# Top-k attention and a SmeLU MLP on one core: paired top-k, earlier exponentials, SmeLU off VectorE

## The chip, the cores and the metric

The kernel runs on one core of a Trainium2 chip, in one launch. The metric is the device time of that launch in microseconds (us). The engines are named as in the profile: PE (TensorE), PEld (its weight loads), DVE (VectorE), ACT (ScalarE), POOL (GpSimd) and SP (SyncE, which only issues transfers here).

## The reference

Eight batches of eight heads, 576 positions, head size 64. For every query the 32 largest scores are kept, a softmax is taken over them, and the result is multiplied by the values. The heads are put side by side (4608 tokens of 512) and go through a two-layer MLP with SmeLU between:

```
scores = q @ k.T / sqrt(64)
kth    = 32nd largest of each row;  mask = scores >= kth
attn   = exp(where(mask, scores, -1e9) - max);  attn /= sum(attn) + 1e-9
x      = (attn @ v), heads side by side            # 4608 x 512
h      = x @ w_in                                  # 512 x 2048
g      = h if h >= 1, 0 if h <= -1, else (h + 1)^2 / 4
out    = g @ w_out                                 # 2048 x 512
```

q, k and v are float32. The two weight matrices come as float64, and the kernel turns their 64-bit words into float32 on the chip.

## The kernel before

**Steps.** The attention is cut into 144 steps. A step is one tile of 128 query rows for two heads, so it holds two score blocks of 128 x 576 (tile `s`, i = 0 and 1). The leftover 64 rows of each head are paired into tail steps of the same size. Step m passes through `scores` (PE matmuls into PSUM, four ACT copies to `s`), `top_k` (DVE: four rounds of MAX8 and between them three of MATCH_REPLACE8, on each of the two blocks, 576 wide), `weights` (POOL makes the negated 32nd value `nkth` and a bias `nb`; ACT masks with a steep Prelu, then Exp with a running sum `z`; DVE adds 1e-9 and takes the reciprocal `rz`; POOL multiplies by it), `transpose_w` (PE transposes, ACT copies to `wT`) and `values` (PE, then an ACT copy to `xT`).

**The MLP.** Query tiles are gathered into chunks of two (sometimes one). When a chunk's attention is done, `mlp` puts 16 pieces `hidden(f)` and, for each tile, 8 pieces `final` into a list. `hidden(f)` makes `ph` in PSUM (3 buffers), then ACT makes r = relu(h/2 + 1/2), POOL squares it, and DVE writes g = min(max(h, 1), r^2), reading `ph`. `r` has 2 buffers. `final` accumulates g @ w_out in `py`.

**Weights.** `weight_piece` turns 512 columns at a time of float64 words into float32: three DVE operations, two on ACT, two on POOL, and a last one on DVE (line 98). 32 pieces are needed, three in each step from the start; a `hidden` or `final` piece may be issued only when the columns that it reads have been converted.

**Order.** PE's order is written out by hand: in iteration m the loop issues `values(m-2)`, `scores(m+1)`, half of the step's share of MLP pieces, `transpose_w(m-1)`, and the other half. The share is the MLP work that is left over the steps that are left. The order of the other engines is chosen by a scheduler when the program is built; each engine then runs its own list strictly in order, and waits on semaphores for the others and for itself.

Of the kernel before, what the change touches and what calls it, by code (L numbers as in the profile page):

```python
# [16 lines left out]
TOP_K = 32  # L17
# [4 lines left out]
def kernel(  # L22
# [29 lines left out]
    FAR = 2.0 ** 80  # L52
    PER_STEP = 3

    const = ctx.enter_context(tc.tile_pool(name="const", bufs=1))
    xtp = ctx.enter_context(tc.tile_pool(name="xtp", bufs=3))
    stage = ctx.enter_context(tc.tile_pool(name="stage", bufs=2))
    att = ctx.enter_context(tc.tile_pool(name="att", bufs=2))
    ps = ctx.enter_context(tc.tile_pool(name="ps", bufs=1, space=PSUM))

# [3 lines left out]
    nc.gpsimd.memset(half, 0.5)  # L64
    w_in = const.tile([P, NK, DFF], F32, name="w_in")
# [10 lines left out]
    WC = 512  # L76

    def weight_piece(pool, dst, src):
# [5 lines left out]
        top = pool.tile([P, WC], U32, name="top")  # L84
# [10 lines left out]

        size = pool.tile([P, WC], F32, name="size")
        nc.scalar.activation(size, hi.bitcast(F32), AF.Abs)
        nc.vector.scalar_tensor_tensor(out=dst, in0=size, scalar=1.125 * 2.0 ** -15, in1=low,  # L98
                                       op0=ALU.is_ge, op1=ALU.mult)

    def weight_pieces(pool):
        for c in range(0, DFF, WC):
            for kk in range(NK):
                weight_piece(pool, w_in[:, kk, c:c + WC], moe_w_in[kk * P:(kk + 1) * P, c:c + WC])
                yield
        for f in range(NF):
            for c in range(0, DM, WC):
                weight_piece(pool, w_out[:, f, c:c + WC], moe_w_out[f * P:(f + 1) * P, c:c + WC])
                yield
# [4 lines left out]
    def whole(x, b):  # L114

        return x[b, :, 0:SM, :].rearrange("h (p c) d -> p h c d", c=NT)

    def load_values(b):
        v_in = stage.tile([P, H, NT, D], F32, name="v_in")
        nc.sync.dma_start(out=v_in, in_=whole(v, b))  # L120
        v_tl = v_tails[b % 2]
        for j in range(2):
            nc.sync.dma_start(out=v_tl[0][j * TL:(j + 1) * TL, j::2, :],
                              in_=v[b, j::2, SM:S, :].rearrange("h p d -> p h d"))
        for hp in range(NHP):
            g = hp % 2
            nc.sync.dma_start(out=v_tl[1][g * TL:(g + 1) * TL, 2 * hp:2 * hp + 2, :],
                              in_=v[b, 2 * hp:2 * hp + 2, SM:S, :].rearrange("h p d -> p h d"))
        return v_in, v_tl

    def load_queries(b, t):
        if t < NT:
            q_in = stage.tile([P, H, D], F32, name="q_in", bufs=2)
            nc.sync.dma_start(out=q_in, in_=whole(q, b)[:, :, t, :])
        else:
            q_in = stage.tile([TL, H, D], F32, name="q_tl", bufs=2)
            nc.sync.dma_start(out=q_in, in_=q[b, :, SM:S, :].rearrange("h p d -> p h d"))
# [247 lines left out]
    for got in keys_of(0):  # L385
        keys[0] = got
# [78 lines left out]
```

## Time and profile before

| | us |
|---|---|
| median of 3 runs (lowest, highest) | 2017.13 (2016.01, 2020.04) |
| the profiled execution, its span | 2018.67, 2016.9 |
| busy: PE, PEld | 1717.6, 1175.6 |
| busy: DVE, ACT, POOL | 1608.3, 1075.0, 537.6 |

The profile is of one execution. Busy time is the union of an engine's instructions, and instructions of DVE, ACT and POOL overlap their neighbours a little, so what an instruction costs in a queue is the distance from its start to the next one's start. The view of waits and the `<-` at the end of a row name what ended the idle time in front of an instruction.

### The profile page before, as it was taken

Reading aid. Unit: us, or ns where it says so; the run is one execution under the profiler, and the core shown is the slowest. Engines: PE = TensorE matmul, PEld = TensorE weight load, DVE = VectorE, ACT = ScalarE, POOL = GpSimd, SP = SyncE. Lnnn points to the kernel's source line nnn. Section 1 sums busy time; section 2 is a strip of 40 time slices with the busy share of each in tenths; the row PEclk is TensorE's granted clock in tenths of the full one; section 3 lists DMA queues with packets and bytes.
Section 4 is the critical chain, followed back from the end, with each engine's and each line's share of the span. In section 5 each row is a group of like instructions: output and inputs, shape, how many; then the busy total and the mean of one; then the engine's idle time right before and its main releaser. Section 6 shows DMA issues by size and latency. Waiting matters only on the chain.

```text
span 2016.9 us, 29329 instructions
## 1 busy us (share of the span) xinstructions
PE 1717.6 (85%) x10128; PEld 1175.6 (58%) x10128; DVE 1608.3 (80%) x3648; ACT 1075.0 (53%) x2589; POOL 537.6 (27%) x1003
## 2 busy tenths in 40 slices
PE   3245488989989999989898999888999999998999
PEld 2243266557566666656565666656474765765666
DVE  4878789989897887889786887888787787968861
ACT  4545546565555654565555555565454555545442
POOL 2564522213221221213121222213131231321321
PEclk7667798999999999989998999999999999999999
DMA  6232200100011001100011000110010000000000
GB/s 162 78 92 75 68 14 18 41 22 12 21 30 30 22 3 29 33 22 11 21 30 29 22 1 23 28 35 11 14 33 21 17 6 11 6 16 6 1 11 11
DMA packets 102803, 57.45 MB, mean 28 GB/s; under 512 B 85760, under 2 KB 93952, under 8 KB 102656
## 3 DMA queue, kind: packets, MB, share of 16 engines
q1 hardware_dynamic: 102656, 55.59, 10.0%
q8 instruction: 80, 1.31, 0.3%
q14 instruction: 67, 0.55, 0.1%
HBM read 46.14 MB, written 9.44 MB: 28 GB/s over the span
## 4 chain that ended last, share of the span: by engine, by line
DVE 53%; PE 19%; ACT 12%; POOL 10%; issue 6%; DMA 1%; SPq 0%; POOLq 0%; DVEq 0%; ACTq 0%
DVE tops L218 27%; DVE rest L221 20%; PE py L315 9%; PE ph L300 4%; ACT s L228 4%; ACT s L239 3%; DVE g L307 3%; POOL s L244 3%; ACT s L209 2%; POOL r L306 2%; PE sp L206 2%; POOL low L93 2%; PE po L269 2%; POOL low L94 2%; PE pw L254 2%
## 5 line engine op out<-in xcount | busy, mean ns | idle before, releaser
L300 PE MATMUL ph<-xT,w_in 128*128 128x256 f32 (+1 forms) x2816 | 560.4, 355 | 72.0 <-DVE g L307 71.8
L218 DVE MAX8 tops<-rest 128x8 f32<-128x576 f32 x864 | 619.5, 748 | 0.1
L315 PE MATMUL py<-w_out,g 128*128 128x512 f32 x1152 | 558.6, 630 | 45.1 <-DVE w_out L98 39.5
L300 PEld LDWEIGHTS ph<-xT,w_in 128*128 128x128 f32 x2816 | 466.2, 197 | 158.0 <-DVE g L307 87.9
L221 DVE MATCH_REPLACE8 rest<-tops,rest 128x576 f32<-128x576 f32 x576 | 424.1, 743 | 0.0
L315 PEld LDWEIGHTS py<-w_out,g 128*128 128x128 f32 x1152 | 217.5, 199 | 306.1 <-issue 238.0
L228 ACT ACTIVATE s<-s,nkth 128x576 f32<-128x576 f32 x288 | 214.4, 772 | 315.4 <-POOL nkth L233 315.2
L218 DVE MAX8 tops<-s 128x8 f32<-128x576 f32 x288 | 205.9, 750 | 202.7 <-ACT s L209 202.7
L244 POOL TENSOR_SCALAR s<-s,rz 128x576 f32<-128x576 f32 x288 | 217.6, 768 | 382.0 <-DVE rz L242 243.1
L306 POOL TENSOR_TENSOR r<-r 128x256 f32<-128x256 f32 (+1 forms) x352 | 187.8, 540 | 423.6 <-ACT r L304 418.4
L206 PE MATMUL sp<-kT,qT 64*128 64x288 f32 x1024 | 196.8, 452 | 60.2 <-ACT xT L282 51.2
L304 ACT ACTIVATE r<-ph,half 128x256 f32<-128x256 f32 (+1 forms) x352 | 148.2, 433 | 172.8 <-PE ph L300 141.3
L255 ACT COPY wT<-pw 128x512 f32<-128x512 f32 x288 | 155.9, 587 | 132.8 <-PE pw L254 131.7
L239 ACT ACTIVATE s<-s,nb 128x576 f32<-128x576 f32 x288 | 221.6, 770 | 1.2
L254 PE MATMUL pw<-ident,s 128*128 128x128 f32 x1152 | 163.5, 288 | 68.8 <-POOL s L244 64.1
L209 ACT ACTIVATE s<-sp 128x288 f32<-128x288 f32 x576 | 198.7, 410 | 36.3 <-PE sp L206 34.7
L221 DVE MATCH_REPLACE8 rest<-tops,s 128x576 f32<-128x576 f32 x288 | 212.6, 743 | 0.0
L254 PEld LDWEIGHTS pw<-ident,s 128*128 128x128 f32 x1152 | 142.9, 149 | 119.5 <-POOL s L244 72.6
L307 DVE SCALAR_TENSOR_TENSOR g<-ph,r 128x256 f32<-128x256 f32 (+1 forms) x352 | 128.6, 368 | 76.4 <-POOL r L306 71.3
L233 POOL TENSOR_SCALAR nkth<-tops 128x2 f32<-128x2 f32 x144 | 29.1, 202 | 571.1 <-DVE tops L218 571.1
L206 PEld LDWEIGHTS sp<-kT,qT 64*128 64x128 f32 x1024 | 108.4, 194 | 108.0 <-ACT xT L282 66.0
L269 PEld LDWEIGHTS po<-wT,v_in 128*64 128x64 f32 x2048 | 120.1, 143 | 85.6 <-issue 41.3
(51 smaller groups left out, 1086.7 us busy)
## 6 DMA issues: line engine op xcount, KB each, us to landing
q_in<-in_q_dram SPq DMA_DIRECT2D x32, 256.0 KB, 3.1
v_in<-in_v_dram SPq DMA_DIRECT2D x8, 1024.0 KB, 5.9
k_in<-in_k_dram SPq DMA_DIRECT2D x64, 128.0 KB, 3.2
raw<-in_moe_w_in_dram SPq DMA_DIRECT2D x16, 512.0 KB, 3.9
raw<-in_moe_w_out_dram SPq DMA_DIRECT2D x16, 512.0 KB, 3.5
out_dram<-y SPq DMA_DIRECT2D x32, 256.0 KB, 2.3
v_tail<-in_v_dram SPq DMA_DIRECT2D x16, 64.0 KB, 2.5
k_tl<-in_k_dram SPq DMA_DIRECT2D x8, 128.0 KB, 3.2
```

The costliest lines, as they stand in the source:

```text
L206: nc.tensor.matmul(o[:, a0 - c0:a1 - c0], qT[d, g, :], kT[d, g, k0:k0 + a1 - a0], start=True, stop=True)
L209: nc.scalar.activation(s[:, i, c0:c1], sp[i], AF.Copy, scale=SCALE)
L218: nc.vector.max(out=tops[:, i, r:r + 8], in_=src[:, i, :])
L221: nc.vector.match_replace(out=rest[:, i, :], in_to_replace=tops[:, i, r:r + 8], in_values=src[:, i, :], imm_value=LOWEST)
L228: nc.scalar.activation(x, x, AF.Prelu, bias=nkth, alpha=FAR)
L239: nc.scalar.activation(s[:, i, :], s[:, i, :], AF.Exp, bias=nb[:, i:i + 1], accum_out=z[:, i:i + 1])
L244: nc.gpsimd.tensor_scalar(s[:, i, :], s[:, i, :], rz[:, i:i + 1], 1.0, ALU.mult, ALU.mult)
L254: nc.tensor.transpose(pt[:, c, :], w[:, i, main(i)][:, c * P:(c + 1) * P], ident)
L300: nc.tensor.matmul(ph, w_in[:, kk, f * P:(f + 1) * P], xT[:, kk, 0:cw], start=(kk == 0), stop=(kk == NK - 1))
L306: nc.gpsimd.tensor_tensor(out=r, in0=r, in1=r, op=ALU.mult)
L307: nc.vector.scalar_tensor_tensor(out=g[:, 0:cw], in0=ph, scalar=1.0, in1=r, op0=ALU.max, op1=ALU.min)
L315: nc.tensor.matmul(py, gs[f][:, i * P:(i + 1) * P], w_out[:, f, :], start=(f == 0), stop=(f == NF - 1))
```

## The change

1. **Paired top-k.** The 576 scores of a row are folded into 288 pairs. `more` holds the larger of each pair, `less` the smaller. The four rounds of MAX8 and MATCH_REPLACE8 run on `more`, 288 wide. Then the 8 largest of `less` are taken (`seconds`), and the 32nd largest of both lists together follows from 8 minima and one more MAX8 per block (`kth`). This is exact unless 8 members of `less` lie above the result; by how much the 8th does is kept in `excess`.
2. **A general path.** At the end the largest `excess` is reduced to one flag, which all engines read. If it is positive, the whole attention and MLP run again without pairing. The code of that second pass is in the program in any case.
3. **Exponentials.** Exp is taken of all 576 scores with the row's maximum as bias, right after the first round of MAX8, into a new tile `e`. The mask, the product and the sum are one DVE instruction per block (line 271, `SCALAR_TENSOR_TENSOR` with an accumulated `z`). The Prelu on ACT is gone.
4. **SmeLU.** g = min(relu((h+1)/2), 1)^2 + relu(h-1): two ACT operations that read `ph`, then three on POOL (clip, square, add). DVE has no part in it.
5. **Weights.** The pieces are 256 wide, so there are 64 of them, with two buffers for each temporary. The last DVE operation of a piece is issued behind the next piece's first three. Four pieces are issued ahead of step 0, then six in each step, between the parts of `weights`.
6. **Order.** DVE's order is written out by hand too, as the program issues it. `wT`, `wTt` and `q_tl` have one buffer where they had two.

```diff
-    WC = 512
+    WC = 256
...
-        top = pool.tile([P, WC], U32, name="top")
+        top = pool.tile([P, WC], U32, name="top", bufs=2)
...
         nc.scalar.activation(size, hi.bitcast(F32), AF.Abs)
+        yield
         nc.vector.scalar_tensor_tensor(out=dst, in0=size, scalar=1.125 * 2.0 ** -15, in1=low,
                                        op0=ALU.is_ge, op1=ALU.mult)
...
+        def weights(st, between):
...
+            if paired:
+                more = att.tile([P, 2, SH], F32, name="more", bufs=1)
+                less = att.tile([P, 2, SH], F32, name="less", bufs=1)
+                nc.vector.tensor_tensor(out=more, in0=s[:, :, 0:SH], in1=s[:, :, SH:S], op=ALU.max)
+                src = rest = more
+            else:
+                src, rest = s, att.tile([P, 2, S], F32, name="rest", bufs=1)
+            for r in range(0, TOP_K, 8):
+                for i in range(2):
+                    nc.vector.max(out=tops[:, i, r:r + 8], in_=src[:, i, :])
+                if r == 0:
+                    nc.gpsimd.tensor_scalar(nmax, tops[:, :, 0], -1.0, 1.0, ALU.mult, ALU.mult)
+                    for i in range(2):
+                        nc.scalar.activation(e[:, i, :], s[:, i, :], AF.Exp, bias=nmax[:, i:i + 1])
+                if r + 8 < TOP_K:
+                    for i in range(2):
+                        nc.vector.match_replace(out=rest[:, i, :], in_to_replace=tops[:, i, r:r + 8],
+                                                in_values=src[:, i, :], imm_value=LOWEST)
+                    src = rest
+                between()
+            if paired:
+                nc.vector.tensor_tensor(out=less, in0=s[:, :, 0:SH], in1=s[:, :, SH:S], op=ALU.min)
...
             for i in range(2):
+                nc.vector.scalar_tensor_tensor(out=e[:, i, :], in0=s[:, i, :], scalar=last[:, i:i + 1],
+                                               in1=e[:, i, :], op0=ALU.is_ge, op1=ALU.mult,
+                                               accum_out=z[:, i:i + 1])
+            between()
...
+                nc.scalar.activation(g[:, 0:cw], ph, AF.Relu, bias=minus, scale=1.0)
+                nc.gpsimd.tensor_scalar(r, r, 1.0, 0.0, ALU.min, ALU.max)
+                nc.gpsimd.tensor_tensor(out=r, in0=r, in1=r, op=ALU.mult)
+                nc.gpsimd.tensor_tensor(out=g[:, 0:cw], in0=r, in1=g[:, 0:cw], op=ALU.add)
...
+        order = tc.manual_schedule(engines={mybir.EngineType.PE, mybir.EngineType.DVE})
...
+    again = nc.values_load(flag[0:1, 0:1], min_val=0, max_val=1)
+    with tc.If(again > 0):
+        with ExitStack() as inner:
+            run(inner, False)
```

On DVE, one whole step without weight pieces, before (`tops` and `rest` belong to the top-k, `z` and `rz` to the step ahead of it):

```order
L218 MAX tops<-s 128x8 x2
L221 MATCH_REPLACE rest<-tops,s 128x576 x2
L241 TENSOR_SCALAR z<-z 128x2
L218 MAX tops<-rest 128x8
L242 RECIPROCAL rz<-z 128x2
L218 MAX tops<-rest 128x8
L221 MATCH_REPLACE rest<-tops,rest 128x576 x2
L218 MAX tops<-rest 128x8 x2
L221 MATCH_REPLACE rest<-tops,rest 128x576 x2
L218 MAX tops<-rest 128x8 x2
```

and now, where every row belongs to one step:

```order
L238 TENSOR_TENSOR more<-s 128x576
L244 MAX tops<-more 128x8 x2
L251 MATCH_REPLACE more<-tops,more 128x288 x2
...
L244 MAX tops<-more 128x8 x2
L256 TENSOR_TENSOR less<-s 128x576
L259 MAX seconds<-less 128x8 x2
L260 TENSOR_TENSOR tops<-tops,seconds 128x2x8
L263 MAX kth<-tops 128x8 x2
L271 SCALAR_TENSOR_TENSOR e,z<-s,kth,e 128x576 x2
L276 TENSOR_SCALAR z<-z 128x2
L277 RECIPROCAL rz<-z 128x2
```

`z` and `rz` now close their own step on DVE. Four instructions still pass over 576 elements (`more` and `less`, which take both blocks at once, and line 271 twice), where all fourteen did.

On ACT, between two tail steps of the MLP's hidden part, before (`s<-s,nkth` is the mask, `s,z<-s,nb` the exponential, `s<-sp` the copies of the next step's scores):

```order
L284 COPY xT<-po 128x2x64
L209 ACTIVATE s<-sp 128x288 x4
L228 ACTIVATE s<-s,nkth 128x576 x2
L239 ACTIVATE s,z<-s,nb 128x576 x2
L304 ACTIVATE r<-ph,half 128x256 x3
L255 COPY wT<-pw 128x512 x2
```

and now:

```order
L318 COPY xT<-po 128x128
L224 ACTIVATE s<-sp 128x288 x4
L340 ACTIVATE r<-ph,half 128x256
L342 ACTIVATE g<-ph,minus 128x256
...
L291 COPY wT<-pw 128x512 x2
L294 COPY wTt<-pwt 128x128
L248 ACTIVATE e<-s,nmax 128x576 x2
```

The mask that waited for the end of a step's top-k is gone from ACT's list. The exponential, which waits only for the first round, stands behind the `wT` copies of the step before.

On POOL, in a step of the MLP's hidden part, before:

```order
L306 TENSOR_TENSOR r<-r 128x256 x2
L244 TENSOR_SCALAR s<-s,rz 128x576 x2
L306 TENSOR_TENSOR r<-r 128x256 x3
L233 TENSOR_SCALAR nkth<-tops 128x2
L235 TENSOR_TENSOR nb<-tops 128x2
```

and now:

```order
L343 TENSOR_SCALAR r<-r 128x256
L344 TENSOR_TENSOR r<-r 128x256
L345 TENSOR_TENSOR g<-r,g 128x256
L264 TENSOR_TENSOR excess<-seconds,kth 128x2
L343 TENSOR_SCALAR r<-r 128x256
L344 TENSOR_TENSOR r<-r 128x256
L345 TENSOR_TENSOR g<-r,g 128x256
L279 TENSOR_SCALAR e<-e,rz 128x576
L343 TENSOR_SCALAR r<-r 128x256
L279 TENSOR_SCALAR e<-e,rz 128x576
```

Each hidden piece has three POOL instructions where it had one, and the products with `rz` stand between them.

## Rows read from the trace of the kernel before

**Rows 1.** The page, parts 1 and 4: busy time, and the chain by engine.
```profile
PE 1717.6 (85%) x10128; PEld 1175.6 (58%) x10128; DVE 1608.3 (80%) x3648; ACT 1075.0 (53%) x2589; POOL 537.6 (27%) x1003
...
DVE 53%; PE 19%; ACT 12%; POOL 10%; issue 6%; DMA 1%; SPq 0%; POOLq 0%; DVEq 0%; ACTq 0%
```

**Rows 2.** Windows: length, busy time (instructions) by engine, granted clock, DMA share.
```profile
0.00:250.00 250.00, 107.82 (x574) 76.06 (x574) 183.79 (x386) 118.52 (x254) 117.02 (x134) 0.71 0.33 95
250.00:1971.00 1721.00, 1567.80 (x9320) 1071.58 (x9319) 1419.55 (x3245) 946.24 (x2311) 412.70 (x852) 0.96 0.07 19
1971.00:2017.00 46.00, 41.94 (x238) 28.00 (x237) 5.00 (x18) 10.21 (x27) 7.83 (x18) 0.98 0.03 12
```

**Rows 3.** The same windows of line 242 alone (one per step).
```profile
0.00:250.00 250.00, 1.67 (x11) 0.71 0.33 95
250.00:1971.00 1721.00, 20.09 (x132) 0.96 0.07 19
```

**Rows 4.** Groups on DVE from 250 to 1971 us: busy, mean ns, idle before.
```profile
L218 DVE MAX8 tops<-s 128x8 f32<-128x576 f32 x266 | 189.6, 749 | 200.7 <-ACT s L209 200.7
L307 DVE SCALAR_TENSOR_TENSOR g<-ph,r 128x256 f32<-128x256 f32 x224 | 92.5, 416 | 37.3 <-POOL r L306 33.0
L307 DVE SCALAR_TENSOR_TENSOR g<-ph,r 128x128 f32<-128x128 f32 x96 | 26.9, 282 | 12.7 <-POOL r L306 12.0
```

**Rows 5.** Timeline of DVE near 1000 us: start, length, instruction.
```profile
1000.14 0.74 DVE L218 MAX8 tops<-rest 128x8 f32<-128x576 f32 x1
1000.80 0.41 DVE L307 SCALAR_TENSOR_TENSOR g<-ph,r 128x256 f32<-128x256 f32 x1
1001.12 0.75 DVE L218 MAX8 tops<-s 128x8 f32<-128x576 f32 x1
1001.79 0.07 DVE L221 MATCH_VALUE_LOAD rest<-tops,s 128x8 f32 x1
1001.85 0.74 DVE L221 MATCH_REPLACE8 rest<-tops,s 128x576 f32<-128x576 f32 x1
```

**Rows 6.** Timeline of DVE near 20 us, where each needs the one ahead.
```profile
20.19 0.43 DVE L85 TENSOR_SCALAR top<-raw 128x512 uint32<-128x512 uint32 x1 [20.19 <-DMA raw<-in_moe_w_in_dram]
20.65 0.69 DVE L86 SCALAR_TENSOR_TENSOR top<-raw,top 128x512 uint32<-128x512 uint32 x1
```

**Rows 7.** Groups on POOL, all of the span.
```profile
L244 POOL TENSOR_SCALAR s<-s,rz 128x576 f32<-128x576 f32 x288 | 217.6, 768 | 382.0 <-DVE rz L242 243.1 <-ACT s L209 38.3 <-ACT wTt L258 35.3
L306 POOL TENSOR_TENSOR r<-r 128x256 f32<-128x256 f32 x224 | 135.7, 612 | 302.2 <-ACT r L304 297.1 <-DVE rz L242 5.0
L93 POOL TENSOR_TENSOR low<-low,unit 128x512 f32<-128x512 f32 x32 | 40.7, 1271 | 83.2 <-DVE unit L90 36.0 <-ACT size L97 18.8 <-ACT s L239 13.2
```

**Rows 8.** Timeline of DVE and POOL from 94 to 98 us.
```profile
94.44 1.27 POOL L93 TENSOR_TENSOR low<-low,unit 128x512 f32<-128x512 f32 x1 [2.19 <-ACT s L239]
95.11 0.62 DVE L241 TENSOR_SCALAR z<-z 128x2 f32<-128x2 f32 x1
97.03 2.16 POOL L244 TENSOR_SCALAR s<-s,rz 128x576 f32<-128x576 f32 x2
97.08 0.69 DVE L98 SCALAR_TENSOR_TENSOR w_in<-size,low 128x512 f32<-128x512 f32 x1 [0.55 <-POOL low L94]
```

**Rows 9.** Timelines of PE in three steps.
```profile
660.95 1.09 PE L269 MATMUL po<-wT,v_in 128*64 128x128 f32 x16
663.36 1.16 PE L300 MATMUL ph<-xT,w_in 128*128 128x128 f32 x8
664.36 3.60 PE L315 MATMUL py<-w_out,g 128*128 128x512 f32 x8
...
1001.77 1.04 PE L254 MATMUL pw<-ident,s 128*128 128x128 f32 x8
1002.76 1.89 PE L300 MATMUL ph<-xT,w_in 128*128 128x256 f32 x8
1010.29 3.72 PE L300 MATMUL ph<-xT,w_in 128*128 128x256 f32 x16
```

More of the change, by code (lines that the diff above doesn't have):

```diff
@@ L105, in weight_pieces @@
+        before = None
+        for dst, src in pieces:
+            piece = weight_piece(pool, dst, src)
+            next(piece)
+            if before is not None:
+                next(before, None)
                 yield
[L106 to L109, printed above, removed]
+            before = piece
+        next(before, None)
+        yield
     n_pieces = NK * DFF // WC + NF * DM // WC
-    def whole(x, b):
-        return x[b, :, 0:SM, :].rearrange("h (p c) d -> p h c d", c=NT)
@@ new lines, in run, with convert, advance @@
+        pieces_left = weight_pieces(mlp_pool)
+        pending = deque()
+        total, spent = sum(len(tiles) for tiles in chunks) * (NK * NF + NF * DM // P), 0
+        converted, due = (0 if paired else n_pieces), 0.0
+        def convert():
+            nonlocal converted
+            if converted < n_pieces:
+                converted += 1
+                next(pieces_left)
+        def advance(amount):
+            nonlocal spent, due
+            due += amount
+            while pending and pending[0][1] <= converted and due >= pending[0][0]:
+                cost, _, work = pending.popleft()
+                due -= cost
+                spent += cost
+                work()
+            due = min(due, 8.0)
@@ new lines, in begin @@
+        def begin(m):
+            b, t, hp, ch, col = steps[m]
+            if ch not in xTs:
+                xTs[ch] = xtp.tile([P, NK, CW], F32, name="xT")
+            state.append(dict(m=m, t=t, hp=hp, keys=keys[b], qT=qTs[b, t], xT=(xTs[ch], col)))
+            scores(state[m])
+        queries(0)
+        begin(0)
+        for _ in range(4):
+            convert()
+        next_keys = 1
+        for m in range(n + 2):
+            if 2 <= m:
+                values(state[m - 2])
+                state[m - 2] = None
+                for ch in [c for c in range(len(chunks)) if ready[c] == m - 2]:
+                    pending.extend(mlp(xTs[ch], chunks[ch], mlp_pool))
+            share = (total - spent) / (n + 2 - m)
+            if m + 1 < n:
+                begin(m + 1)
+            if m < n:
+                weights(state[m], convert)
+            advance(share / 2)
+            if 1 <= m <= n:
+                transpose_w(state[m - 1])
+            queries(m + 2)
+            if m < n and prep is None and next_keys < B and steps[m][0] == next_keys - 1 and steps[m][1] >= 1:
+                prep = keys_of(next_keys)
+            if prep is not None and m % 2 == 0:
+                got = next(prep, None)
+                if got is None:
+                    prep, next_keys = None, next_keys + 1
+                else:
+                    keys[next_keys] = got
+            advance(share / 2)
@@ new lines, in run @@
+        while pending:
+            advance(8.0)
+        order.__exit__(None, None, None)
+    with ExitStack() as inner:
+        run(inner, True)
+    flag = const.tile([1, 8], I32, name="flag")
+    with tc.tile_pool(name="end", bufs=1) as end, tc.tile_pool(name="endps", bufs=1, space=PSUM) as endps:
+        worst = end.tile([P, 8], F32, name="worst")
+        nc.vector.max(out=worst, in_=excess)
+        pt = endps.tile([1, P], F32, name="pt")
+        nc.tensor.transpose(pt, worst[:, 0:1], ident)
+        top = end.tile([1, 8], F32, name="top8")
+        nc.vector.max(out=top, in_=pt)
+        nc.vector.tensor_scalar(flag, top, 0.0, None, ALU.is_gt)
```

504 lines of the change are left out of this document (222 added, 282 removed).

## The prediction

> **What bounds the kernel now.** I read the page first, then the three stretches, then DVE's groups, and last the timelines, for the distance between neighbours. DVE has 53% of the chain and is busy 80% of the span, PE 19% and 85% [rows 1]: two engines near their limits. The stretches separate the causes [rows 2, 3]. Up to 250 us the weights are converted: 11 steps pass, over 20 us each, PE is idle more than half of the time and is granted 0.71 of its clock. From 250 to 1971 us there are 132 steps of 1721/132 = 13.04 us; in each PE is busy 1567.8/132 = 11.9 and DVE 1419.6/132 = 10.75, at a granted clock of 0.96. The last 46 us are the MLP of the last chunk. So in the long stretch both are near their limit and neither reaches it. DVE's largest wait is for fresh scores, 200.7 us or 1.5 us a step [rows 4]. They come late because PE does, and PE comes late partly because `ph` is freed only when DVE, between top-k instructions, gets to g.
>
> **What a DVE instruction costs.** By the distance between starts, 576 elements take 0.66 us, 256 take 0.32, and the value load ahead of a MATCH_REPLACE8 0.06 [rows 5]. That is 0.34 us for 320 elements, so 288 elements take 0.36. No 288-wide MAX8 stands in the trace; its price lies between the 256-wide instruction's 0.32 and half of 0.75 (0.38), which for sixteen of them is -0.6 to +0.3 us a step. An instruction that needs the one just ahead starts 0.03 after its end instead of 0.08 before it, a loss of 0.12 [rows 6].
>
> **Change 1 and 3 on DVE.** Before, a step takes 8 x 0.66 + 6 x 0.72 + 0.13 (z and rz, at the 0.06 that stays when the length is taken off) = 9.73 us, and g adds (224 x 0.33 + 128 x 0.19)/144 = 0.69: 10.4. After: `more` 0.78 (0.66 and a dependence); eight MAX8 2.88; six MATCH_REPLACE8 at 0.42, 2.52; `less` 0.78; `seconds` 0.84; minima 0.20; `kth` 0.27; line 271 twice 1.32, with 0.12 for the dependence and 0.14 for reading two sums; z and rz 0.27. Together 10.1 us. So halving the top-k (9.6 to 5.4) is nearly eaten by what the pairing and the mask add, and DVE's own list gets only 0.3 us shorter. Line 271 with its sum is not in the trace: its lower bound is 0.66, as any 576-wide instruction, its upper one twice that, if the sum takes turns with the inputs. I take 0.66, since line 98, with two SBUF inputs too, costs 0.69 for 512 [rows 8].
>
> The Trainium skill speaks against the change here. "Vector Engine (DVE) Microarchitecture Reference", section "Points that are easy to get wrong", says that this kind of instruction runs at half rate when both sources lie in SBUF and are not bf16, and names the readout of the accumulator. Line 98 has two such sources and runs at the full rate, but it reads out no sum, so the row does not settle it for line 271; what it would make of the time is the third rival.
>
> **What no longer waits.** The mask stood in ACT's list until a step's top-k was done; the exponential that replaces it needs only the first round, and its 1.5 us lie beside the 8 us of DVE work up to line 271. The scores of the next steps stand ahead of it. So the 1.5 us per step that DVE waited for scores go, as far as PE is not late for another reason. If that cover fails, line 271 waits for `e`, and `more` behind it.
>
> **Change 4: SmeLU goes to POOL.** One TENSOR_TENSOR of 256 takes 0.61 and a TENSOR_SCALAR of 576 0.77, so about 0.4 for 256 [rows 7]. A hidden piece thus takes 0.4 + 2 x 0.61 + 0.14 for two dependences = 1.76 us on POOL, where it took 0.61. PE makes one in 3.72/2 = 1.86 [rows 9]. ACT gains a 256-wide relu per piece and loses the mask; it was busy 55% of the stretch [rows 2], so I cost that at nothing.
>
> POOL and DVE also get in each other's way. A two-element instruction of DVE that started at 95.11 took 0.62, where line 242, as small, takes 20.09/132 = 0.15, and ended with POOL's product [rows 3, 8]; two POOL multiplications, 0.77 each on average, took 2.16 when line 98 started beside the first [rows 7, 8]. Plain top-k instructions do not show it. I read this as exclusion between POOL and those DVE instructions that read two SBUF tensors or run a fast mode. The change brings DVE five of them per step (`more`, `less`, the minima, line 271 twice) beside z: 0.74 + 0.74 + 0.16 + 1.5 + 0.16 = 3.3 us.
>
> **The step after.** PE: `values` and `scores` 2.41 and the transposes 0.99 [rows 9]. The MLP is 224 x 1.86 + 128 x 1.00 + 288 x 1.80 = 1063 us, some 60 of it in the first stretch, so 1003/133 = 7.5 a step. That is 10.9, or 11.3 at a granted clock of 0.96. The share of a step is about four MLP pieces, either all hidden or all final:
> - Hidden steps, half of them: POOL has 4 x 1.76 + 1.5 (products with rz) + 0.5 = 9.0 us, and with DVE's 3.3 that is 12.3 us of exclusive time. DVE has 10.1 plus waits of about 0.4 at each of six instructions, 12.5. Both lists lean on each other; I take 12.8.
> - Final steps: POOL has 2 us, DVE 10.1 + 0.3, so PE sets the pace: 11.5.
>
> The mean is 12.15 us, against 13.04.
>
> **Change 5: the first stretch.** A 256-wide piece costs DVE 0.31 + 0.45 + 0.20 + 0.33 = 1.3 us, six per step 7.8: with 10.1 that is 17.9. POOL's twelve products (0.61 each) and the exclusion add some 2.5; and the last instruction of the piece that closes a step waits, in DVE's now fixed list, for ACT's copies behind `wT` and `e`, about 2 us. Ten steps of 22.4 are 224, and 30 us pass ahead of step 0 (five pieces stand in front of it): 254, against 250 for one step more. Bounds: 17.9 and 26 per step, 210 to 290. On SP the 64 loads of 256 columns wait for the same readers as the 32 before, with two in flight either way; I count nothing.
>
> **Change 2 and the end.** Worked out from the inputs that the reference sets up: in no row do more than 6 pairs have both members among the 32, where the general path needs at least 8, and the 8th of `less` stays at least 0.0009 below the result. So the second pass does not run. MAX8 over `excess`, a transpose, another MAX8, a comparison and a load by every engine stand behind the last matmul, beside the last copy and transfer: 0 to 10 us, I take 5. The last chunk's hidden pieces go from 0.9 apart to about 1.1 on POOL, 2 us: 46 + 7 = 53.
>
> **Sum.** 254 + 133 x 12.15 + 53 = 1923, and the profiled execution lay 1.8 above its span (2018.67 and 2016.9), 1.5 above the median of 2017.13. Forecast: 1925 us, 4.6% faster.
>
> **Rivals.**
> 1. The exclusion hides and PE sets the pace in all steps: 11.4 us. For it: POOL's first instruction of a piece often waits for ACT anyway, and DVE's plain instructions leave POOL 6.8 us of a step. Against it: 9.0 us of POOL work do not fit there in hidden steps. 133 x 11.4 + 245 + 52 + 2 = 1815.
> 2. POOL becomes the bound (slower). In hidden steps every one of DVE's six instructions waits for a whole POOL instruction (0.6 each, 13.7), and with `r` in 2 buffers ACT stands in its list behind POOL, so the `wT` copies and `e` come late as well: 15 us; final steps start late, 12. The mean is 13.5: 133 x 13.5 + 262 + 55 = 2113. It decides from a mean of (2017 - 254 - 55)/133 = 12.85 on, only 0.7 above what I take. For it: the rows of the lock. Against it: half of the steps have hardly any POOL work.
> 3. Line 271 at half rate: 2 x 0.6 = 1.2 us more per step, on DVE and in the exclusive time. Hidden steps 14.0, final ones 11.9, mean 12.95: 133 x 12.95 + 262 + 55 = 2039. For it: the sum; against it: line 98.
> 4. The change does not do what it says, because the flag is raised: a whole second pass of at least 144 x 11, 3,500 us in all. The inputs speak against it.
>
> **Chances.** Forecast (1870 to 1980) 0.51, first rival 0.18, second 0.20, third 0.10, fourth 0.01. A measurement of this kernel can tell about 0.2%, or 4 us, from no change. The forecast and the first rival are faster, the second and fourth slower, the third mostly slower: faster 0.71, same 0.04, slower 0.25. The range takes in the first rival and the third, and of the second what lies up to a mean of 13.2: 1800 to 2075. The forecast's own range is 1870 to 1980.
>
> **What would show it.** Right: MAX8 and MATCH_REPLACE8 0.36 apart; DVE's wait for scores nearly gone; POOL busy about 45% of the span (0.8 ms); line 271 0.66 apart when POOL rests and longer when it does not; hidden steps longer than final ones by over 1 us; PE busy over 90% in final steps. Wrong: line 271 at 1.2 us (third rival), PE waiting mostly for POOL's or ACT's hidden part and a mean step over 12.85 (second), a mean below 11.6 (first), or a first stretch far from 254 us.

## The result, and the profile after

The kernel after takes 1919.39 us (median of 4 runs, 1915.05 to 1920.87), beside 2018.35 for the kernel before (4 runs, 2016.01 to 2020.04): a ratio of 0.951, 95% interval 0.949 to 0.953. The forecast of 1925 us and its direction held; the reason given for it held only in part.

The page of after, parts 1 and 4, answers to [rows 1].

```profile
PE 1679.1 (88%) x10129; PEld 1160.1 (61%) x10129; DVE 1625.4 (85%) x5011; ACT 977.1 (51%) x2429; POOL 1028.8 (54%) x1772
...
PE 53%; DVE 22%; POOL 13%; ACT 6%; issue 5%; DMA 1%; POOLq 0%; SPq 0%; DVEq 0%; ACTq 0%
```

DVE had 53% of the chain and PE 19%; now it is the other way round, though DVE is busier than before. The windows of after (length, busy time and instructions by engine, granted clock, DMA share) answer to [rows 2]:

```profile
0.00:251.00 251.00, 99.94 (x526) 67.65 (x526) 216.03 (x584) 108.31 (x278) 148.13 (x225) 0.70 0.34 95
251.00:1858.00 1607.00, 1533.33 (x9346) 1062.51 (x9348) 1408.05 (x4424) 854.28 (x2108) 861.13 (x1498) 0.98 0.08 21
1858.00:1913.00 55.00, 45.78 (x260) 29.96 (x259) 1.30 (x5) 14.48 (x43) 19.58 (x51) 0.95 0.03 12
```

Ten steps lie in the first 251 us, 134 in the long stretch, 1607/134 = 11.99 us each where they took 13.04. PE is busy in 95% of it (91% before), and its granted clock is 0.98 (0.96). Of the 1.05 us by which a step got shorter, 0.61 is idle time of PE ((1721 - 1567.8)/132 before, (1607 - 1533.3)/134 now). The rest is PE's busy time, with nearly the same matmuls, as its `py` groups show in the two long stretches:

```profile
L315 PE MATMUL py<-w_out,g 128*128 128x512 f32 x1073 | 514.8, 625 | 7.1 <-ACT y L319 5.6 <-DVE w_out L98 1.5
L353 PE MATMUL py<-w_out,g 128*128 128x512 f32 x1070 | 489.5, 600 | 9.8 <-DVE w_out L99 5.3 <-ACT y L357 4.6
```

So a part of the gain came with shorter matmuls at a higher granted clock; no run tells it apart from the waits. A timeline of DVE in a final step of after (start, length, instruction) shows the new list:

```profile
940.39 0.76 DVE L238 TENSOR_TENSOR more<-s 128x576 f32<-128x576 f32 x1 [1.79 <-ACT s L224]
...
941.99 0.44 DVE L251 MATCH_REPLACE8 more<-tops,more 128x288 f32<-128x288 f32 x1
942.35 0.08 DVE L251 MATCH_VALUE_LOAD more<-tops,more 128x8 f32 x1
...
948.86 0.82 DVE L271 SCALAR_TENSOR_TENSOR e<-s,kth,e 128x576 f32<-128x576 f32 x1
949.62 0.08 DVE L271 DVE_READ_ACCUMULATOR e<-s,kth,e 128x1 f32 x1
949.62 0.81 DVE L271 SCALAR_TENSOR_TENSOR e<-s,kth,e 128x576 f32<-128x576 f32 x1
...
950.67 0.17 DVE L277 RECIPROCAL rz<-z 128x2 f32<-128x2 f32 x1
```

A 288-wide instruction takes 942.35 - 941.99 = 0.36 us of the queue, line 271 takes 0.76 with its sum, and the list from `more` to `rz` 950.67 - 940.39 = 10.3. The wait for scores in its first row is DVE's largest in the whole stretch. Here are waits on DVE and ACT from 251 to 1858 us (engine, line, waited for; total, times, longest):

```profile
DVE more L238 <- ACT s L224: 138.6, 68, 8.5
...
ACT r L340 <- POOL g L345: 115.8, 112, 3.2
```

Fresh scores are waited for 138.6 us (200.7 before, [rows 4]). A new wait stands on ACT: it cannot write `r` before POOL has freed one of its two buffers. PE's own waits, from 250 to 1971 us of before:

```profile
PE sp L206 <- ACT xT L282: 54.3, 33, 5.1
...
PE ph L300 <- DVE g L307: 41.0, 30, 4.3
```

and from 251 to 1858 us of after:

```profile
PE sp L221 <- ACT xT L318: 26.1, 23, 5.2
```

The wait for `ph` went from 41.0 to 2.8 us (now for ACT's g) and the one for `xT` was halved.

### The profile page after: what moved, and what is told of

Read it like the earlier page. It is cut to its first block, busy times and chain, and to the rows that moved or that the text cites. A ratio compares the mean times of both kernels' runs of the same rounds, so it can differ in the third digit from the quotient of the medians.

```text
span 1913.0 us, 32251 instructions
## 1 busy us (share of the span) xinstructions
PE 1679.1 (88%) x10129; PEld 1160.1 (61%) x10129; DVE 1625.4 (85%) x5011; ACT 977.1 (51%) x2429; POOL 1028.8 (54%) x1772
## 3 DMA queue, kind: packets, MB, share of 16 engines
q1 hardware_dynamic: 107264, 55.59, 10.6%
## 4 chain that ended last, share of the span: by engine, by line
PE 53%; DVE 22%; POOL 13%; ACT 6%; issue 5%; DMA 1%; POOLq 0%; SPq 0%; DVEq 0%; ACTq 0%
PE py L353 24%; PE ph L336 11%; PE sp L221 6%; DVE tops L244 6%; PE po L305 5%; DVE more L251 5%; PE pw L290 4%; POOL g L345 4%; POOL r L344 3%; POOL e L279 2%; POOL r L343 2%; DVE e L271 2%; DVE more L238 2%; DVE seconds L259 2%; DVE less L256 1%
## 5 line engine op out<-in xcount | busy, mean ns | idle before, releaser
L244 DVE MAX8 tops<-more 128x8 f32<-128x288 f32 x1152 | 468.5, 448 | 5.0
L251 DVE MATCH_REPLACE8 more<-tops,more 128x288 f32<-128x288 f32 x864 | 375.9, 443 | 0.0
L279 POOL TENSOR_SCALAR e<-e,rz 128x576 f32<-128x576 f32 x288 | 242.4, 850 | 130.9 <-DVE rz L277 104.9
L271 DVE SCALAR_TENSOR_TENSOR e<-s,kth,e 128x576 f32<-128x576 f32 x288 | 242.4, 875 | 23.1 <-ACT e L248 6.6
L345 POOL TENSOR_TENSOR g<-r,g 128x256 f32<-128x256 f32 (+1 forms) x352 | 246.7, 701 | 24.0
L290 PE MATMUL pw<-ident,e 128*128 128x128 f32 x1152 | 161.5, 284 | 110.6 <-POOL e L279 105.9
L248 ACT ACTIVATE e<-s,nmax 128x576 f32<-128x576 f32 x288 | 213.1, 786 | 75.2 <-POOL nmax L246 74.4
L238 DVE TENSOR_TENSOR more<-s 128x576 f32<-128x576 f32 x144 | 130.4, 905 | 139.0 <-ACT s L224 138.6
L290 PEld LDWEIGHTS pw<-ident,e 128*128 128x128 f32 x1152 | 138.0, 146 | 162.5 <-POOL e L279 118.2
L343 POOL TENSOR_SCALAR r<-r 128x256 f32<-128x256 f32 (+1 forms) x352 | 155.4, 441 | 93.5 <-ACT r L340 93.2
```

The source lines that it names most:

```text
L244: nc.vector.max(out=tops[:, i, r:r + 8], in_=src[:, i, :])
L248: nc.scalar.activation(e[:, i, :], s[:, i, :], AF.Exp, bias=nmax[:, i:i + 1])
L251: nc.vector.match_replace(out=rest[:, i, :], in_to_replace=tops[:, i, r:r + 8], in_values=src[:, i, :], imm_value=LOWEST)
L271: nc.vector.scalar_tensor_tensor(out=e[:, i, :], in0=s[:, i, :], scalar=last[:, i:i + 1], in1=e[:, i, :], op0=ALU.is_ge, op1=ALU.mult, acc ...
L279: nc.gpsimd.tensor_scalar(e[:, i, :], e[:, i, :], rz[:, i:i + 1], 1.0, ALU.mult, ALU.mult)
L290: nc.tensor.transpose(pt[:, c, :], w[:, i, main(i)][:, c * P:(c + 1) * P], ident)
```

## The experiments

Four theories were set against each other. P: PE sets the pace of the long stretch, and the change takes PE's waits away. D: DVE's list sets it, and what shortens the list counts. L: in hidden steps the exclusion of POOL and DVE sets it, as the prediction had it. A, formed after the first four runs: before was paced by ACT's in-order list, where the mask waits for the end of the top-k; after by PE.

Each kernel was timed beside before, whose median was 2017.0 to 2019.8 us throughout. The step columns are worked out from each trace: distances between starts of the `rz` reciprocal, from the tenth step on, by the PE matmuls between them (hidden: three or more pieces of `ph`, wide for chunks of two tiles; final: three or more pieces of `py` and less than one of `ph`; the rest is mixed and in the mean only).

| kernel | us, ratio to before (95%) | 10th step ends | wide hidden | one-tile hidden | final | mean of 134 |
|---|---|---|---|---|---|---|
| before | 2018.35 | 227 | 12.80 | 16.00 | 13.18 | 13.02 |
| after | 1919.39, 0.951 (0.949-0.953) | 251 | 11.58 | 14.94 | 11.86 | 11.99 |
| b_smelu | 2094.41, 1.036 (1.033-1.040) | 229 | 13.50 | 16.84 | 13.60 | 13.54 |
| b_exp | 1977.79, 0.980 (0.977-0.982) | 237 | 13.29 | 15.00 | 11.57 | 12.63 |
| b_pair | 1999.42, 0.991 (0.989-0.994) | 213 | 12.98 | 16.23 | 12.96 | 12.94 |
| b_xt_dve | 2010.03, 0.997 (0.995-0.998) | 226 | 12.93 | 16.38 | 12.40 | 12.95 |
| a_auto | 1888.86, 0.936 (0.933-0.938) | 245 | 11.44 | 15.23 | 11.83 | 11.86 |
| a_unpaired | 1938.18, 0.960 (0.959-0.962) | 260 | 12.02 | 14.20 | 11.82 | 12.11 |
| a_smelu_dve | 2140.12, 1.060 (1.058-1.062) | 265 | 16.52 | 21.15 | 10.57 | 13.67 |
| a_smelu_dve_auto | 1859.69, 0.922 (0.919-0.924) | 240 | 11.97 | 14.76 | 10.88 | 11.66 |
| a_less_pool | 1841.37, 0.912 (0.911-0.914) | 248 | 11.11 | 13.37 | 11.57 | 11.51 |
| a_r4 | 1875.86, 0.930 (0.928-0.933) | 252 | 11.55 | 13.63 | 11.43 | 11.71 |
| a_half_final | 1799.37, 0.892 (0.889-0.894) | 251 | 11.45 | 12.78 | - | 11.23 |
| a_hi_dve_auto | 1783.89, 0.883 (0.882-0.885) | 166 | 12.05 | 14.51 | 10.90 | 11.66 |

Between two `rz` a final step does not hold the same PE work in every kernel: it has 18.4 `py` matmuls in before, 17.7 in after, 16.9 in b_exp and a_r4, at 0.45 us each [rows 9]. So differences of a few tenths in these columns can be PE work that falls to another step. A second table cuts the same traces at PE, from the first matmul of one `values` to that of the next. Then a final step holds 17.9 `py` matmuls and a wide hidden one 36.7 of `ph` in all of these kernels; one-tile steps hold 60.0 of `ph` in the kernels made from before and 62.4 in those made from after.

| kernel, cut at PE | wide hidden | one-tile hidden | final |
|---|---|---|---|
| before | 13.87 | 14.89 | 13.82 |
| b_exp | 14.60 | 14.55 | 12.03 |
| b_xt_dve | 14.43 | 15.55 | 12.64 |
| after | 13.72 | 14.74 | 11.96 |
| a_unpaired | 13.32 | 14.80 | 11.96 |
| a_less_pool | 13.06 | 13.22 | 11.80 |
| a_r4 | 13.48 | 13.34 | 11.84 |

By this cut the change takes 1.9 us from a final step and 0.15 from a hidden one. Where the two tables differ, what follows goes by the second.

### One part at a time, on the kernel before

b_smelu puts `Relu` on ACT and clip, square and add on POOL in place of DVE's g.

```diff
+            nc.scalar.activation(g[:, 0:cw], ph, AF.Relu, bias=minus, scale=1.0)
+            nc.gpsimd.tensor_scalar(r, r, 1.0, 0.0, ALU.min, ALU.max)
             nc.gpsimd.tensor_tensor(out=r, in0=r, in1=r, op=ALU.mult)
-            nc.vector.scalar_tensor_tensor(out=g[:, 0:cw], in0=ph, scalar=1.0, in1=r, op0=ALU.max, op1=ALU.min)
+            nc.gpsimd.tensor_tensor(out=g[:, 0:cw], in0=r, in1=g[:, 0:cw], op=ALU.add)
```

> The kernel before, with the fourth part of the change alone: the SmeLU's second half on ScalarE and GpSimd instead of VectorE. Theory P (TensorE sets the pace of the long stretch, and what the change gives is the waits of TensorE that it takes away): the 72 us of ph <- DVE g and most of the 88 us of weight loads behind it go, and the higher clock comes with it, so 1940 to 1975 us. Theory D (VectorE's list sets the pace): the list loses 0.69 us of 10.4 a step, some 95 us over 139 steps, 1910 to 1930 us. Theory L (GpSimd's and VectorE's exclusion sets the hidden steps): GpSimd's two more instructions a piece lock VectorE's ten wide ones, 1990 to 2050 us.

It is 75 us slower, past every theory; L's 1990 to 2050 came nearest. Waits in its long stretch, from 229 to 2044 us:

```profile
DVE tops L220 <- ACT s L211: 354.0, 99, 8.6
...
PE sp L208 <- ACT xT L284: 91.6, 57, 4.4
...
ACT r L306 <- POOL g L311: 82.6, 76, 3.2
...
PE ph L302 <- ACT g L308: 10.3, 10, 3.3
```

PE's wait for `ph` went (41.0 to 10.3 us) as P said, but its wait for `xT` rose from 54.3 to 91.6 and DVE's for scores from 200.7 [rows 4] to 354.0. So the length of DVE's list was not the bound (it is busy 10.0 us a step in place of 10.8). The waits that grew are for `xT` and `s`, which ACT hands on, and ACT now waits for POOL to free `r` as well. That these, and not the exclusion of theory L, cost the time is argued from the waits; no run takes one of them away from b_smelu.

b_exp takes the Prelu mask off ACT, moves the exponential up behind the first round, and puts mask, product and sum on DVE. `wT`, `wTt` and `q_tl` have one buffer each.

```diff
+                for i in range(2):
+                    nc.scalar.activation(e[:, i, :], s[:, i, :], AF.Exp, bias=nmax[:, i:i + 1])
...
-            mask(s[:, i, :], nkth[:, i:i + 1])
-            nc.scalar.activation(s[:, i, :], s[:, i, :], AF.Exp, bias=nb[:, i:i + 1], accum_out=z[:, i:i + 1])
+            nc.vector.scalar_tensor_tensor(out=e[:, i, :], in0=s[:, i, :], scalar=tops[:, i, TOP_K - 1:TOP_K],
+                                           in1=e[:, i, :], op0=ALU.is_ge, op1=ALU.mult,
+                                           accum_out=z[:, i:i + 1])
```

> The kernel before, with the third part alone: the exponentials during the top-k, mask, product and sum on VectorE; the top-k stays on 576 columns, and wT, wTt and q_tl have one buffer each to make room. VectorE's list grows by two instructions of some 0.8 us a step. Theory P: 139 steps keep TensorE's pace as long as the list stays under it, and the later g costs some of that: 2000 to 2070 us. Theory D: plus 1.6 us in each of 139 steps, about 2240 us.

It is 42 us faster, better than both theories, though DVE is busy 12.2 us a step in place of 10.8. Its long stretch, and DVE's wait for scores there:

```profile
237.00:1929.00 1692.00, 1547.60 (x9351) 1073.35 (x9352) 1632.16 (x3821) 769.94 (x1796) 410.15 (x732) 0.96 0.08 21
```

```profile
DVE tops L218 <- ACT s L209: 13.6, 9, 4.9
```

The wait for scores is all but gone, and final steps fall from 13.82 to 12.03 us with the same PE work. DVE is now the bound, busy 1632.16/1692 = 96%, and wide hidden steps get longer, 14.60 for 13.87. b_exp takes from ACT at once the wait for the end of the top-k and 1.4 us of work a step (946.24/132 to 769.94/134); no run has one without the other.

b_pair folds the scores into pairs and keeps everything else.

```diff
+        nc.vector.tensor_tensor(out=more, in0=s[:, :, 0:SH], in1=s[:, :, SH:S], op=ALU.max)
+        src = rest = more
...
-        nc.gpsimd.tensor_scalar(nkth, tops[:, :, TOP_K - 1], -1.0, 1.0, ALU.mult, ALU.mult)
+        nc.gpsimd.tensor_scalar(nkth, kth[:, :, 0], -1.0, 1.0, ALU.mult, ALU.mult)
```

> The kernel before, with the paired top-k alone (the eight largest out of 288 maxima, the minima merged behind them; no general path). VectorE's list is some 1.3 us a step shorter. Theory P: the stretch where VectorE is dense (the first ten steps) gains 1.3 us each, the long one a little by an earlier g: 1970 to 2010 us. Theory D: minus 1.3 us in each of 149 steps, 1820 to 1850 us.

P's range held: 20 us, 14 of them before the tenth step ends; the long stretch goes from 13.02 to 12.94 us a step only, though DVE is busy 69% of the span (80% before).

What held those steps stands in the trace of before itself, in final steps near 960 us (timelines of ACT, PE and DVE):

```profile
954.53 0.26 ACT L258 COPY wTt<-pwt 128x128 f32<-128x128 f32 x1
960.56 1.44 ACT L228 ACTIVATE s<-s,nkth 128x576 f32<-128x576 f32 x2 [5.77 <-POOL nkth L233]
961.91 0.76 ACT L239 ACTIVATE s<-s,nb 128x576 f32<-128x576 f32 x1
962.58 0.19 ACT L239 ACTIVATION_READ_ACCUMULATOR s<-s,nb 128x1 f32 x1
962.67 0.24 ACT L282 COPY xT<-po 128x128 f32<-128x128 f32 x1
...
962.96 0.75 PE L206 MATMUL sp<-kT,qT 64*128 64x288 f32 x2 [3.42 <-ACT xT L282]
...
964.30 0.17 DVE L241 TENSOR_SCALAR z<-z 128x2 f32<-128x2 f32 x1 [4.12 <-ACT s L239]
```

ACT stood 5.77 us at the mask, because the mask needs the end of the top-k. Behind it stood the copy of `po`, whose buffer the scores use too. So PE waited 3.42 us, and DVE, once its top-k was done, 4.12 us for what ACT had not yet made. Theory A says that this, not DVE's list, paced before. ACT's waits at the mask over the long stretch, in before and then in b_pair, fit it: the shorter top-k leaves them as they are.

```profile
ACT s L228 <- POOL nkth L233: 292.3, 115, 7.3
ACT s L240 <- POOL nkth L245: 288.5, 125, 5.9
```

b_xt_dve moves only that copy.

```diff
-            nc.scalar.copy(xT[:, hp, col:col + P], po)
+            nc.vector.tensor_copy(xT[:, hp, col:col + P], po)
...
```

> The kernel before, with nothing changed but the engine that copies po to xT: VectorE instead of ScalarE. Theory A (before is paced by ScalarE's list: the mask waits there for the end of the top-k, and the xT copy behind it holds po's buffer, which the next scores need): TensorE's 123 us of waits for xT go for the most part, and 1960 to 2000 us result. Theory D (VectorE's list sets the pace): 0.2 us more in each of 144 steps, 2020 to 2060 us.

Between the theories: 7 us faster. Final steps fall by 1.2 us as A says, wide hidden ones rise by 0.6, and PE still waits for the copy, now behind DVE's top-k (36.4 us in place of 54.3). One copy alone does not show A; b_exp, which removes the mask itself, is the stronger sign.

### One part taken back, from the kernel after

a_auto leaves DVE's order to the scheduler.

```diff
-        order = tc.manual_schedule(engines={mybir.EngineType.PE, mybir.EngineType.DVE})
+        order = tc.manual_schedule(engines={mybir.EngineType.PE})
```

> The kernel after without its written order on VectorE: the tile scheduler places VectorE's instructions as before, TensorE's order stays. Theory P: between 0 and 30 us slower than after, since TensorE sets the pace and any order that gives e in time will do. Theory D and L: an order that puts the mask and the exclusion elsewhere moves the time by over 40 us in one direction.

It is 31 us faster, which P had put on the other side. Of the 24 us between the two profiled executions, 6 lie in the first stretch and 18 in the long one. The written order costs time; which of its places does was not tried apart.

a_unpaired runs the top-k on all 576 columns.

```diff
+            paired = False
```

> The kernel after, with the top-k over all 576 columns (no pairs, no minima): VectorE's list is 1.3 us a step longer, about 11.4. Theory A (TensorE paces after, VectorE close behind it): the list is now over TensorE's pace in the hidden steps, where GpSimd lengthens it by waits, and just under it in the final ones: 1950 to 2000 us. Theory D: 1.3 us in each of 144 steps, 2100 us. Theory L (the exclusion between GpSimd and VectorE's instructions with two inputs sets the hidden steps): three such instructions fewer a step pay for most of the longer list, 1920 to 1950 us.

19 us slower, below the range of A and inside that of L. 9 us go before the tenth step. After it DVE is busy 11.7 us a step in place of 10.5, and a step takes 0.12 more in the mean: PE's pace covers the rest. Cut at PE, final and one-tile steps are unchanged and wide hidden ones 0.4 shorter; between two `rz` the wide ones are 0.44 longer and the one-tile ones 0.74 shorter. As the cuts disagree, the classes say nothing for or against L.

a_smelu_dve gives g back to DVE, in the written order; a_smelu_dve_auto does so and leaves the order to the scheduler.

```diff
-                nc.scalar.activation(g[:, 0:cw], ph, AF.Relu, bias=minus, scale=1.0)
-                nc.gpsimd.tensor_scalar(r, r, 1.0, 0.0, ALU.min, ALU.max)
                 nc.gpsimd.tensor_tensor(out=r, in0=r, in1=r, op=ALU.mult)
-                nc.gpsimd.tensor_tensor(out=g[:, 0:cw], in0=r, in1=g[:, 0:cw], op=ALU.add)
+                nc.vector.scalar_tensor_tensor(out=g[:, 0:cw], in0=ph, scalar=1.0, in1=r, op0=ALU.max, op1=ALU.min)
```

> The kernel after, with the SmeLU of before (one GpSimd square, VectorE writes g and frees ph). Theory A: VectorE's list is 0.7 us longer and TensorE waits for ph again in the hidden steps: 1930 to 1970 us. Theory L: GpSimd's work in hidden steps falls from about 9 to 4.3 us and the exclusion with it, 1840 to 1890 us. Theory D: 0.7 us in each of 144 steps, about 2015 us.

> The kernel after with the SmeLU of before, and VectorE's order left to the scheduler (so: the paired top-k, the early exponentials and the narrower weight pieces together, without the other two parts). Theory A (with the mask off ScalarE's list and the top-k paired, VectorE's list of some 10.9 us fits under TensorE's pace; the 221 us that the SmeLU on VectorE cost under the written order are VectorE standing at g for GpSimd): 1890 to 1940 us. Theory S (it is the SmeLU's move that takes TensorE's waits away, in either order): TensorE waits for ph as before, 1980 us or more.

The first is 221 us slower than after, far beyond all three theories; the second is 60 us faster than after, beyond A's range. DVE's waits in the long stretch, in the written order:

```profile
DVE g L343 <- POOL r L342: 327.7, 200, 8.9
```

and in the scheduler's:

```profile
DVE more L238 <- ACT s L224: 66.5, 38, 6.4
DVE g L343 <- POOL r L342: 55.6, 83, 2.2
```

In the written order DVE stands at g until ACT and POOL have made `r`, and hidden steps take 16.5 us. There 278 of the 352 g stand right behind another g, between two steps' top-k; the scheduler puts all but 23 singly between other instructions. So moving the SmeLU is worth 221 us under the written order, and costs 29 under the scheduler's (1888.86 against 1859.69). The two parts together, order and SmeLU, cost 60 us: what made after faster than before is the exponentials and the pairing. (The narrower weight pieces ran with them and in no run alone; their work ends with the tenth step, at 240 us against 227 in before.) a_smelu_dve_auto computes everything and beats both kernels.

a_less_pool leaves one POOL instruction a piece.

```diff
-                nc.gpsimd.tensor_scalar(r, r, 1.0, 0.0, ALU.min, ALU.max)
-                nc.gpsimd.tensor_tensor(out=r, in0=r, in1=r, op=ALU.mult)
```

> The kernel after without the clip and the square of the SmeLU on GpSimd (left out, so that g is relu(h - 1) + (h + 1) / 2 cut at zero): one GpSimd instruction a piece instead of three. Theory A: TensorE paces the hidden steps anyway; only the steps of single-tile chunks, 14.9 us each, get shorter, by some 2 us in 12 of them, and the last pieces a little: 1885 to 1915 us. Theory L: the hidden half of the steps falls from GpSimd's pace to VectorE's, over 1 us each: 1820 to 1860 us.

78 us faster, so POOL's work does cost; A's range was missed here and L's held. But wide hidden steps gave 0.66 us, not L's 1, and one-tile ones 1.5. a_r4 tells the way:

```diff
-                r = pool.tile([P, CW], F32, name="r", bufs=2)[:, 0:cw]
+                r = pool.tile([P, CW], F32, name="r", bufs=4)[:, 0:cw]
```

> The kernel after with r of the SmeLU in four buffers instead of two. Theory A (what GpSimd's long SmeLU costs comes over ScalarE: its list stands still until GpSimd frees r, 116 us in the long stretch, and the copies to xT and wT behind it come late): that wait goes, and 1870 to 1900 us result. Theory L (it comes over VectorE, whose two-input instructions wait for GpSimd's): nothing of this changes, 1910 to 1925 us.

44 of the 78 us come with POOL's work unchanged. ACT's wait and the stretch in a_r4:

```profile
ACT r L340 <- POOL g L345: 19.9, 28, 1.4
```

```profile
252.00:1820.00 1568.00, 1511.68 (x9344) 1053.78 (x9344) 1409.12 (x4421) 855.14 (x2108) 861.38 (x1490) 0.98 0.08 21
```

ACT's wait falls from 115.8 to 19.9 us, one-tile steps by 1.4, wide hidden ones by 0.2, and POOL and DVE are as busy as in after. In a_less_pool the same wait falls to 24.5 us. So more than half of what the clip and the square cost goes over ACT's list (A). The other 34 us fit L, but no run separates them from an earlier g.

### What paces after

a_half_final takes PE work away from final steps, and touches no other engine's.

```diff
-                for f in range(f0, f1):
+                for f in range(f0 + 1, f1):
...
-                                     start=(f == 0), stop=(f == NF - 1))
+                                     start=(f == 1), stop=(f == NF - 1))
```

> The kernel after without every second step f of the final matmuls (left out, so that the output holds half of the sum): TensorE has some 265 us less to do, nearly all of it in final steps. Theory A (TensorE paces): final steps fall from 11.9 us to VectorE's floor of 10.3 to 10.6, mixed ones by half as much, the tail by some 20 us: 1800 to 1840 us. Theory D (VectorE's list and its waits pace): only the tail gets shorter, 1890 to 1905 us.

120 us faster, where D allowed 30; 1799.37 is just under the 1800 that A began at. Its long stretch and its chain:

```profile
251.00:1756.00 1505.00, 1360.75 (x8834) 996.61 (x8835) 1403.20 (x4422) 849.89 (x2109) 865.88 (x1497) 0.95 0.08 22
```

```profile
DVE 45%; PE 23%; POOL 15%; issue 8%; ACT 7%; DMA 1%; POOLq 0%; DVEq 0%; SPq 0%; ACTq 0%
```

PE is 173 us less busy, the stretch 102 us shorter with the same DVE work, and the chain is DVE's again (93% busy). PE paces after in the mean, and DVE stands some 0.8 us a step behind it (11.99 - 11.23).

a_hi_dve_auto is a_smelu_dve_auto with half of a weight piece's DVE work and none on ACT and POOL. It leaves out the low 32-bit words of the weights.

```diff
-        top = pool.tile([P, WC], U32, name="top", bufs=2)
+        top = dst.bitcast(U32)
...
-        nc.vector.tensor_scalar(unit, top, 0xFF800000, None, ALU.bitwise_and)
...
-        nc.gpsimd.tensor_tensor(out=low, in0=low, in1=unit.bitcast(F32), op=ALU.mult)
-        nc.gpsimd.tensor_tensor(out=low, in0=low, in1=top.bitcast(F32), op=ALU.add)
...
-        nc.vector.scalar_tensor_tensor(out=dst, in0=size, scalar=1.125 * 2.0 ** -15, in1=low,
-                                       op0=ALU.is_ge, op1=ALU.mult)
```

> The version with the SmeLU of before and the scheduler's order, with the weights made from the high 32-bit words alone (the low words' bits are left out, and the flush of tiny values): two VectorE instructions a weight piece instead of four, none on ScalarE and GpSimd. Theory W (the first stretch is set by VectorE's list, 7.8 us of pieces and 10 of top-k a step, plus what GpSimd's products add): 4.6 + 10.1 us a step and no products, the first ten steps end at 175 to 195 us instead of 240, and 1795 to 1815 us result. Rival (the transfers of the weights or TensorE at its lower clock set that stretch): under 20 us gained there, 1840 us or more.

76 us faster than a_smelu_dve_auto, more than W's 45 to 65. First and long stretch of a_smelu_dve_auto:

```profile
0.00:240.00 240.00, 97.61 (x526) 69.25 (x526) 202.68 (x601) 103.92 (x262) 132.61 (x193) 0.72 0.34 99
240.00:1803.00 1563.00, 1504.28 (x9342) 1047.18 (x9343) 1418.87 (x4743) 760.42 (x1788) 519.62 (x858) 0.99 0.08 21
```

and of a_hi_dve_auto:

```profile
0.00:166.00 166.00, 88.74 (x526) 65.51 (x526) 136.71 (x476) 59.16 (x134) 29.72 (x66) 0.80 0.50 143
166.00:1728.00 1562.00, 1504.09 (x9342) 1045.80 (x9343) 1417.82 (x4741) 760.95 (x1788) 518.85 (x856) 0.99 0.08 21
```

All of it lies in the first stretch, at the same PE work; the transfers, at 50% of the DMA engines in place of 34%, did not hold it back. From the first `rz` (38) to the tenth (166) a step takes 14.2 us, where W had added DVE's list up to 14.7. DVE is busy for 121.0 of these 128.6 us, or 94%. The long stretch is the same to 1 us.

## Why the prediction came out right, step by step

- **First stretch.** 254 us forecast, 251 measured; nine steps between the first `rz` (49 us) and the tenth take 22.4 us each, as the sum had it. Its parts were not as the sum had them, so that the total fits is partly luck. DVE is busy for 189.65 of these 201.9 us, 21.1 a step, which is 3.2 over the plain list of 17.9; the sum took 2.5 there, for POOL's products and the exclusion. The wait of about 2 us for ACT's copies does not show: DVE is idle 1.4 us a step, and what it waits for by name is POOL's `low` (6.3 us in all). a_hi_dve_auto shows that the weight pieces set this stretch; it takes their work from DVE, ACT and POOL at once.
- **DVE's list.** 10.1 us forecast, 10.3 measured; 288 elements 0.36, as taken. Line 271 takes 0.76 and 0.74, its sum's readout included, where the forecast had 0.66 and 0.07. So the third rival falls: the rule of the Trainium skill ("Vector Engine (DVE) Microarchitecture Reference", "Points that are easy to get wrong") that two f32 sources in SBUF halve the rate does not show in this instruction, and nor does a price for the readout beyond 0.08 us.
- **Hidden steps, the step that failed.** "Both lists lean on each other; I take 12.8", against final steps of 11.5. Between two `rz` hidden steps take (44 x 11.58 + 12 x 14.94)/56 = 12.3 in the mean, only 0.4 over the 11.86 of final ones and not over 1. Cut at PE they take (46 x 13.72 + 10 x 14.74)/56 = 13.9 and final ones 11.96, but that is PE's own work: PE is idle for 0.74 us of a wide hidden step and 0.18 of a final one. By neither cut do POOL's and DVE's lists set them. The term mis-sized is "waits of about 0.4 at each of six instructions", 2.4 us a step. The exclusion is there: timelines of DVE and POOL in a hidden step of after.

```profile
466.21 1.00 POOL L344 TENSOR_TENSOR r<-r 128x256 f32<-128x256 f32 x1
466.77 0.45 DVE L276 TENSOR_SCALAR z<-z 128x2 f32<-128x2 f32 x1
467.28 0.72 POOL L345 TENSOR_TENSOR g<-r,g 128x256 f32<-128x256 f32 x1
467.34 1.27 DVE L238 TENSOR_TENSOR more<-s 128x576 f32<-128x576 f32 x1
467.96 0.71 POOL L264 TENSOR_TENSOR excess<-seconds,kth 128x2 f32<-128x2 f32 x1
```

`z` ends when POOL's square ends (0.45 us, 0.17 alone), `more` takes 1.27 (0.76 alone), and POOL's `excess`, of two elements, 0.71 until `more` is through (0.20 alone). But over the 56 hidden steps the mean excess over the undisturbed length is 0.18 us for `more`, 0.05 for `less`, 0.09 for the minima, 0.12 for each line 271 and 0.24 for `z`: 0.8 us a step, a third of what I took. 10.3 + 0.8 stays under PE's pace.
- **The number.** The mean of all, 11.99 for 12.15, is near partly by luck: hidden steps came out below the forecast between two `rz`, final ones above it (11.86 for 11.5), and 34 of the 134 are mixed (11.66), which the sum did not have. The sum also counts 133 steps behind the first ten where 134 stand (144 in all). With 134 the forecast would have been 1937 us; the slip hid 12 of the 21 us by which the long stretch was forecast too long.
- **"The 1.5 us per step that DVE waited for scores go, as far as PE is not late for another reason".** The clause decided: 1.0 us a step is left, since PE now comes later than DVE. The cover of the early exponential held: line 271 waited 6.6 us for `e` in 134 steps. What I did not see is why this part mattered most: before, the mask in ACT's list held back `xT` and the scores (b_exp, b_smelu).
- **Change 4.** "ACT gains ... I cost that at nothing": wrong. ACT's wait for `r` costs 44 us (a_r4). POOL was busy 54% of the span, not 45%; its add takes 0.73 and not 0.61 alone, and the exclusion lengthens its instructions too.
- **PE's pace.** 11.3 us at a clock of 0.96 forecast; PE is busy 11.4 a step in after at 0.98, and a_less_pool comes down to 11.5 a step. The forecast and the first rival both leave out the transposes of queries and keys (`pq` and `pk`, 17.5 + 3.7 + 16.8 + 2.8 = 41 us in the long stretch of after, 0.3 a step). The first rival is the right mechanism, its price of 11.4 a little low: between two `rz` PE is busy for 11.2 us of the 11.58 in wide hidden steps, 11.7 of the 11.86 in final ones and 13.8 of the 14.94 in one-tile ones. The second rival's bound, POOL, holds in none of them (11.2 us of the 14.94). What it said of `r` in 2 buffers does show: with 4 buffers one-tile steps take 13.63 us in place of 14.94 (a_r4), and POOL is still busy for 10.6 us of each.
- **The end.** 53 us forecast, 55 measured; the general path did not run.

## What to carry to other kernels

An engine's in-order list couples work that has no data in common: look for the instruction that waits longest in it and ask what stands behind it. Parts of a change need not add up: alone they gave +75, -42 and -20 us, while exponentials and pairing together, with the new weight pieces, gave 158, because each uncovers the limit that the other removes. A written order can make a part necessary that is a loss without it, so try a part in both orders before its worth is named.

## What the runs showed of the hardware that was not expected

- POOL's f32 add of two 128x256 tiles takes 0.73 us undisturbed, its square of one such tile 0.61.
- The exclusion of POOL and DVE works in both directions, and MAX8 and MATCH_REPLACE8 keep their length beside POOL (0.44 to 0.45 us in hidden and final steps alike).
- The granted clock, a mean over stretches at the two levels of 1.2 and 2.4 GHz, was 0.80 in the first ten steps of a_hi_dve_auto and 0.72 in those of a_smelu_dve_auto, with the same 526 matmuls in 166 and 240 us. By these means PE was at the lower level for some 66 us in a_hi_dve_auto and 134 in a_smelu_dve_auto (an estimate, 2 x (1 - mean) x length). How much of the 76 us that is was not measured apart.
